# Outputs in two transfers of 64 rows, another order of loads, and a reshaped start, in a kernel that fuses linear attention with a two-layer MLP

## The chip, the cores and the metric

One core of a Trainium2 chip runs the whole program. The metric is device time in microseconds (us) of one execution. A run that is over 1.5% above the fastest of its kernel is labelled slow; comparisons use fast runs. The profile is of one execution, and its span is 1.7 us shorter than the time of that execution (220.1 against 221.82 us before).

## The reference, cut to what matters

```python
def _attn_ref(q, k, v, alpha):          # (4, 8, 768, 48): batch, heads, tokens, width
    for t in range(S):
        state = alpha[:, :, t, :, None] * state + outer(k_t, v_t)
        y[:, :, t] = q_t @ state
def _moe_ref(x, w_in, w_out):           # x is y as (3072, 384); w_in (384, 2048), w_out (2048, 384)
    h = x @ w_in
    r = np.maximum(h, 0.0)
    return ((r * r) @ w_out).astype(np.float32)
```

Inputs and the output are float32; the kernel multiplies in bfloat16.

## The kernel before

The work is cut into 12 units of 256 tokens. A unit has a front (decay factors, scaled q and k, their transposes), a back (key-value product `kv`, scores, masking, attention output `y`, its transpose) and an MLP part: 8 first-layer blocks `s1` of 6 matmuls and 8 second-layer groups `s2` of 4. The program records operations with a cost and a priority. A small model in Python then simulates five engines and the transfers, and so fixes, at build time, in which order each engine's queue holds them. On the chip each engine works through its queue in that order and waits on semaphores. What matters later is that an engine does not step over an operation whose data are late.

```python
# the model of time: what a transfer is thought to take
if o.sem is not None:
    dma_free = max(dma_free, o.end + self.DMA_FIRST) + o.lag
    land = dma_free + self.DMA_LAST
# ...  (cut)
# loads of one unit: alpha, k, q, v, 384 KB each, issued by SyncE
load_op[g, nm] = add("sp", lambda e, dst=dst, src=src: e.dma_start(dst, src), 400, L_PRIO[g] + j,
    writes=[("raw", r, j)], name=f"ld{nm}{g}", dma=f"{nm}{r}", lag=1500,
    after=[load_op[AFTER[g]]] if g in AFTER else [])
# ...  (cut) transposes of scaled k (a = 0) and q (a = 1): TensorE for units 0-5, DMA for units 6-11
bank = as_bf16(psZ if a == 0 else psX)
# ...  (cut) the output: one transfer per 128 tokens; partition 64*j + i holds token 2*i + j
r0 = b * S + i * T + 128 * jq
dst = bass.AP(tensor=out.tensor, offset=out.offset + r0 * DM, ap=[[DM, 2], [2 * DM, 64], [1, DM]])
add("sp", lambda e, ob=ob, dst=dst: e.dma_start(dst, OSB[ob][:]), 400, ps_ + 1300,
    reads=[("osb", ob)], name=f"out{m}_{ti}", dma=f"o{ob}", lag=600)
# ...  (cut) which transfer waits for which; win and wout are the weights, in two halves
AFTER = {("win", 0): (0, "q"), ("win", 1): (0, "q"), ("wout", 0): ("win", 0), ("wout", 1): ("win", 0),
         2: ("wout", 0), 3: ("wout", 0), 4: ("wout", 1), 5: ("wout", 1), 6: ("wout", 1)}
```

Of the kernel before, what the change touches and what calls it, by code (L numbers as in the profile page):

```python
# [5 lines left out]
ALU = mybir.AluOpType  # L6
# [253 lines left out]
def pe_ns(count, cols, at_once=1):  # L260
    return count * max(cols / 2.4 + 2.5, 25) / at_once
# [6 lines left out]
def dve_ns(n, rate=1.0):  # L268
    return 150 + n / 0.96 / rate
# [6 lines left out]
def bass_gla_recurrent__then__act_relu_squared_kernel(  # L276
# [9 lines left out]
    B, H, S, D = q.shape  # L286
# [57 lines left out]
    def as_bf16(t):  # L344
        return t[:].rearrange("p a b -> p (a b)").bitcast(BF16) if len(t.shape) == 3 else t[:].bitcast(BF16)
# [13 lines left out]
    def fill(buf, val):  # L359
        return lambda e: e.memset(buf, val)  # L360
# [3 lines left out]
                                         pattern=pattern, channel_multiplier=mult)  # L364

    for i in range(2):
        add("dve", fill(LAB[i][:], 0.0), 300, -1e6, writes=[("lab", i)])
    for i in range(NQKS):
        add("pool" if i else "dve", fill(QKS[i][:].rearrange("p a j h d -> p (a j h d)"), 0.0), 1200, -1e6 + 10,
            writes=[("qks", i, 0), ("qks", i, 1)])  # L370
    add("pool", fill(LINC[:], 1.0), 200, -1e6, writes=[("linc",)])
    add("pool", select(LINC[:], ALU.is_ge, 0.0, 0, [[1, 128]], -1), 300, -1e6, reads=[("linc",)], writes=[("linc",)])
# [11 lines left out]
    add("pool", select(IDENT[:], ALU.not_equal, 1.0, 0, [[-1, 128]], 1), 300, -1e6 + 5, reads=[("ident",)],  # L384
        writes=[("ident",)])

    add("pool", fill(CAUS[:].rearrange("p a b c -> p (a b c)"), 1.0), 200, -1e6 + 7, writes=[("caus",)])
    add("pool", fill(CAUS1[:].rearrange("p a b c -> p (a b c)"), 1.0), 200, -1e6 + 7, writes=[("caus1",)])
    for c, buf, key in ((0, CAUS, "caus"), (1, CAUS1, "caus1")):
        for jk in range(2):  # L390
            add("pool", select(buf[:, jk], ALU.is_ge, 0.0, 128 * c - jk, [[1, 2], [2, 64]], -2), 300, -1e6 + 7,
                reads=[(key,)], writes=[(key,)])
    add("dve", lambda e: e.tensor_copy(CAUS[64:128], CAUS1[64:128]), 200, -1e6 + 8, reads=[("caus1",), ("caus",)],
        writes=[("caus",)])

    def bcast(t, row, dims):
        return bass.AP(tensor=t, offset=0, ap=[[row, 128]] + dims)
# [19 lines left out]
    def load(g):  # L417
        b, i = units[g]
        t0 = i * T
        p0 = g * P  # L420
        r, la, qs, kt, pm, vb, x2 = (g % n for n in (NRAW, 2, NQKS, NKQT, NPM, NV, 2))
        first, last = i == 0, i == NST - 1
        xt = XSLOT[g]
        sr, sw = 2 * b + i % 2, 2 * b + (i + 1) % 2

        for j, t, nm in ((0, alpha, "a"), (1, k, "k"), (2, q, "q"), (3, v, "v")):
            src = t[b, :, t0:t0 + T, :].rearrange("h (p j) d -> p h (j d)", j=2)
            dst = RAW[r][:, j].rearrange("p h j d -> p h (j d)")
            load_op[g, nm] = add("sp", lambda e, dst=dst, src=src: e.dma_start(dst, src), 400, L_PRIO[g] + j,  # L429
                writes=[("raw", r, j)], name=f"ld{nm}{g}", dma=f"{nm}{r}", lag=1500,  # L430
                after=[load_op[AFTER[g]]] if g in AFTER else [])

    def front(g):
        b, i = units[g]
        t0 = i * T
        p0 = (g - AHEAD) * P
        r, la, qs, kt, pm, vb, x2 = (g % n for n in (NRAW, 2, NQKS, NKQT, NPM, NV, 2))
        first, last = i == 0, i == NST - 1
        xt = XSLOT[g]
# [56 lines left out]
        for a in range(2):  # L496
            src = QKS[qs][:, a].rearrange("p j h d -> p (j h d)")
            if g < PE_TRANSPOSED:
                bank = as_bf16(psZ if a == 0 else psX)
                psk = [("ps", "Z" if a == 0 else "X", 0)]  # L500

                def tr(pe, src=src, bank=bank):
                    for o in range(2 * NPR):
                        ins = pe.matmul(bank[:, o * 128:(o + 1) * 128], src[:, o * 128:(o + 1) * 128], IDENT[:],
                                        is_transpose=True)
                    return ins

                add("pe", tr, pe_ns(8, 128), p0 + 2500 + a, reads=[("qks", qs, a), ("ident",)], writes=psk,
                    name=f"tr{a}_{g}")
                dst = KQT[kt][:, a].rearrange("p j n s -> p (j n s)")  # L510
                add("dve", lambda e, dst=dst, bank=bank: e.tensor_copy(dst, bank[:, 0:1024]), dve_ns(1024, 2),  # L511
                    p0 + 3000 + a, reads=psk, writes=[("kqt", kt, a)], name=f"et{a}_{g}",
                    alts={"act": (lambda e, dst=dst, bank=bank: e.activation(dst, bank[:, 0:1024], AF.Copy),
                                  act_ns(1024))})
            else:
                dst = KQT[kt][:, a].rearrange("p j n s -> p (j n) s")
                add("sp", lambda e, dst=dst, src=src: e.dma_start_transpose(dst, src), 500, p0 + 2500 + a,
                    reads=[("qks", qs, a)], writes=[("kqt", kt, a)], name=f"tr{a}_{g}", dma=f"t{a}_{kt}", lag=1100)

    def back(g):  # L520
        b, i = units[g]
# [93 lines left out]
        src = XBF[x2][:].rearrange("p c n -> p (c n)")  # L615
        dst = XT[s][:, slot].rearrange("p c k t -> p (c k) t")
        if g < PE_X:
            bank = as_bf16(psW)

            def xtr(pe):  # L620
                for o in range(2 * KT):
                    ins = pe.matmul(bank[:, o * 128:(o + 1) * 128], src[:, o * 128:(o + 1) * 128], IDENT[:],
                                    is_transpose=True)
                return ins

            add("pe", xtr, pe_ns(6, 128), p0 + 6700, reads=[("xbf", x2), ("ident",)], writes=[("ps", "W")],
                name=f"xt{g}")
            add("dve", lambda e: e.tensor_copy(dst.rearrange("p a t -> p (a t)"), bank[:, 0:768]), dve_ns(768, 2),
                p0 + 7200, reads=[("ps", "W")], writes=[("xt", s, slot)], name=f"xv{g}")
        else:  # L630
            add("sp", lambda e: e.dma_start_transpose(dst, src), 500, p0 + 6700, reads=[("xbf", x2)],
                writes=[("xt", s, slot)], name=f"xt{g}", dma=f"x{s}{slot}", lag=850)

    rr_i = [0]
    h_i = [0]
# [2 lines left out]
    def moe(m, gs):  # L638
# [8 lines left out]
        for u in range(nb):  # L647
            hb, rb = h_i[0] % 2, rr_i[0] % NRR
            h_i[0] += 1
            rr_i[0] += 1  # L650
            pu = p0 + u * W * 0.5 / nb

            def s1(pe, u=u, hb=hb):
                for i in range(per):
                    fj = u * per + i
                    for kk in range(KT):
                        mov = XT[s][:, 0:nu_, :, kk, :].rearrange("p u c t -> p (u c) t")
                        ins = pe.matmul(psH[hb][:, i * n:(i + 1) * n], WIN[:, kk, fj * 128:(fj + 1) * 128], mov,  # L658
                                        start=(kk == 0), stop=(kk == KT - 1))
                return ins  # L660

            fjs = range(u * per, (u + 1) * per)
            add("pe", s1, pe_ns(KT * per, n), pu, reads=[("xt", s, i) for i in range(nu_)]
                + sorted({("win", f // FS) for f in fjs}), writes=[("ps", "H", hb)], name=f"s1_{m}_{u}")
            add("act", lambda e, hb=hb, rb=rb: e.activation(RR[rb][:], psH[hb][:], AF.Relu), act_ns(512), pu + 600,  # L665
                reads=[("ps", "H", hb)], writes=[("rr", rb)], name=f"re{m}_{u}",
                alts={"dve": (lambda e, hb=hb, rb=rb: e.tensor_scalar(RR[rb][:], psH[hb][:], 0.0, None, ALU.max),
                              dve_ns(512))})
            dst = GT[gt][:, u * per:(u + 1) * per, g0:g0 + nu_].rearrange("p f u c t -> p f (u c t)")
            sq = RR[rb][:].rearrange("p (f t) -> p f t", f=per)  # L670
            add("dve", lambda e, dst=dst, sq=sq: e.tensor_tensor(dst, sq, sq, ALU.mult), dve_ns(512, 2), pu + 1200,  # L671
                reads=[("rr", rb)], writes=[("gt", gt, g0 + i, fj) for i in range(nu_) for fj in fjs], name=f"sq{m}_{u}",
                alts={"pool": (lambda e, dst=dst, sq=sq: e.tensor_tensor(dst, sq, sq, ALU.mult), pool_ns(512))})  # L673
        for ti, (ui, jq) in enumerate((ui, jq) for ui in range(nu_) for jq in range(2)):
            b, i = units[gs[ui]]
            ob = o_i[0] % NOSB
# [1 line left out]
            for sg in range(4):  # L678
# [11 lines left out]
            add("act", lambda e, ob=ob: e.activation(OSB[ob][:], psO[:, 0:DM], AF.Copy), act_ns(DM), ps_ + 700,  # L690
                reads=[("ps", "O")], writes=[("osb", ob)], name=f"oe{m}_{ti}",
                alts={"dve": (lambda e, ob=ob: e.tensor_copy(OSB[ob][:], psO[:, 0:DM]), dve_ns(DM))})
            r0 = b * S + i * T + 128 * jq
            dst = bass.AP(tensor=out.tensor, offset=out.offset + r0 * DM, ap=[[DM, 2], [2 * DM, 64], [1, DM]])
            add("sp", lambda e, ob=ob, dst=dst: e.dma_start(dst, OSB[ob][:]), 400, ps_ + 1300,
                reads=[("osb", ob)], name=f"out{m}_{ti}", dma=f"o{ob}", lag=600)

    XSLOT = {g: (m % NXT, ui) for m, gs in enumerate(BLOCKS) for ui, g in enumerate(gs)}
    GSLOT = {}
# [7 lines left out]
    for g in range(5, G):  # L707
        ORDER += [f"f{g}", f"b{g - 1}"]
    ORDER += [f"b{G - 1}"]
    AFTER = {("win", 0): (0, "q"), ("win", 1): (0, "q"), ("wout", 0): ("win", 0), ("wout", 1): ("win", 0),  # L710
             2: ("wout", 0), 3: ("wout", 0), 4: ("wout", 1), 5: ("wout", 1), 6: ("wout", 1)}
    for st in ORDER:
        if st[0] == "f":
            load(int(st[1:]))
# [42 lines left out]
```

## Time and profile before

| before | value |
|---|---|
| time, median of 3 runs | 225.99 us (223.41 to 226.1) |
| span of the profiled run | 220.1 us (its time 221.82) |
| first first-layer matmul starts | 26.65 us |
| last output eviction ends | 210.93 + 0.49 = 211.42 us |
| so: ramp, middle, tail | 26.65, 184.77, 8.7 us |

The page has a view of 40 equal slices (5.5 us each here), one digit per slice: busy tenths for TensorE (PE), granted TensorE clock in tenths, and the mean busy share of the sixteen DMA engines. These are its rows for the kernel before:

```profile
PE   7999999998984998799319999999999999999830
PEclk9999999999998599999965999999999999999995
DMA  6997699999466679556979983457915650400110
```

TensorE is the busy engine, but it dips around slices 10 to 21, its clock drops twice, and the last slices do nothing. The DMA row reads as if there were room in slices 11 to 15 and from slice 25 on, while slices 20 to 24 are nearly full. It is the time that packets took (between 104 and 122 us packets of 256 bytes took 18 ns in median, but up to 3.7 us), as a mean over sixteen engines: whether a few of them have far more to do than the rest cannot be seen in it.

The next view is busy time by stretch of the kernel before: stretch, its length, TensorE busy time and matmul count, clock (1.00 is full), DMA share, GB/s.

```profile
85.00:104.00 19.00, 17.87 (x297) 1.00 0.65 177
104.00:122.00 18.00, 9.97 (x88) 0.72 0.98 169
122.00:135.00 13.00, 12.84 (x168) 1.00 0.76 122
```

In 104 to 122 TensorE loses 8 us and runs part of the rest at half clock. The timeline of SyncE's queue in the kernel before, at that place (start, duration of the issue, what is issued):

```profile
99.48 1.14 SPq L695 DMA_DIRECT2D out_dram<-osb  x1
100.66 1.30 SPq L429 DMA_DIRECT2D raw<-in_alpha_dram  x1
102.00 2.07 SPq L695 DMA_DIRECT2D out_dram<-osb  x1
104.12 4.95 SPq L517 DMA_TRANSPOSE kqt<-qks  x1
109.12 0.58 SPq L429 DMA_DIRECT2D raw<-in_k_dram  x1
109.74 3.30 SPq L517 DMA_TRANSPOSE kqt<-qks  x1
```

and TensorE's timeline there, where the brackets give the idle time before a group and what ended it:

```profile
110.48 0.81 PE L683 MATMUL psO<-wout,gt 128*128 128x384 bf16 x4 [3.85 <-POOL gt L673]
115.47 0.64 PE L573 MATMUL psX<-kqt 64*64 64x128 bf16 x16 [4.18 <-DMA kqt<-qks]
116.05 1.46 PE L658 MATMUL psH<-xt,win 128*128 128x256 bf16 x6
117.30 4.05 PE L683 MATMUL psO<-wout,gt 128*128 128x384 bf16 x12
```

The issue of a transpose blocks SyncE for 4.95 us just behind two outputs, and its tile lands 9.2 us after the start of the issue, the longest landing of the twelve. The transpose behind it is issued at 109.74 and lands 5.69 us later (view of the chain of waits). Afterwards twelve matmuls take 4.05 us where eight take 1.46 at full clock (at 77.49 us).

The ramp, in the timeline of all engines of the kernel before:

```profile
3.58 3.54 POOL L360 MEMSET qks<- 128x2048 bf16 x2
3.66 3.53 DVE L393 COPY caus<-caus 64x256 bf16<-64x256 bf16 x1
7.21 0.56 DVE L445 TENSOR_TENSOR prd<-raw 128x384 f32<-128x384 f32 x1
13.29 0.69 DVE L511 COPY kqt<-psX 128x1024 bf16<-128x1024 bf16 x1 [0.24 <-PE psX L504]
20.12 0.42 PE L573 MATMUL psX<-kqt 64*64 64x128 bf16 x16
21.22 0.83 POOL L485 CAST vbf<-raw 128x768 bf16<-128x768 f32 x1 [11.61 <-DMA raw<-in_v_dram]
26.65 1.47 PE L658 MATMUL psH<-xt,win 128*128 128x256 bf16 x12
```

Unit 0's tiles are ready at 13.98 but its scores run at 20.12, and the first layer starts at 26.65.

### The profile page before, as it was taken

To read this page: it belongs to the slowest core of one execution; us is meant where nothing else is said; L and a number is where in the kernel's file an instruction comes from. 1 tells how busy PE (TensorE), PEld (TensorE's weight loads), DVE (VectorE), ACT (ScalarE), POOL (GpSimd) and SP (SyncE) were. 2 spreads that over 40 slices of the span, in tenths; PEclk is the share of its full clock that TensorE was granted. 3 is DMA by queue.
4 is the path that set the end of the run, shared out by engine and by line. 5 is a ranking of instruction groups with operands and counts; after the bars stand their busy time and mean duration, and the time that the engine had idled before them with its cause. 6 is when DMAs were issued, how large, how long until landed. Compare 5 with 4: busy or idle time off the path is not lost.

```text
span 220.1 us, 5346 instructions
## 1 busy us (share of the span) xinstructions
PE 192.9 (88%) x2317; PEld 130.2 (59%) x2317; DVE 135.5 (62%) x214; ACT 101.7 (46%) x186; POOL 58.4 (27%) x72
## 2 busy tenths in 40 slices
PE   7999999998984998799319999999999999999830
PEld 2354687765662576568205776767677676777510
DVE  7678674893999269599403686884938727142300
ACT  2352185534942155358201555737548364555400
POOL 8701610393625114711313104510301201000000
PEclk9999999999998599999965999999999999999995
DMA  6997699999466679556979983457915650400110
GB/s 177 316 209 159 76 205 277 296 298 275 130 172 166 171 194 289 149 166 173 70 187 248 149 116 64 74 95 87 146 29 88 99 78 27 77 31 27 43 41 35
DMA packets 73416, 31.41 MB, mean 143 GB/s; under 512 B 67504, under 2 KB 72624, under 8 KB 73392
## 3 DMA queue, kind: packets, MB, share of 16 engines
q1 hardware_dynamic: 70512, 27.92, 57.5%
q0 software_dynamic: 2880, 3.15, 8.8%
q8 instruction: 18, 0.29, 0.5%
q14 instruction: 6, 0.05, 0.1%
HBM read 25.17 MB, written 4.72 MB: 136 GB/s over the span
## 4 chain that ended last, share of the span: by engine, by line
PE 63%; DVE 13%; DMA 13%; SPq 3%; issue 2%; ACT 2%; DVEq 0%
PE psO L683 27%; PE psH L658 22%; DMA xt<-xbf 5%; DMA raw<-in_q_dram 5%; DVE qks L490 3%; PE psX L600 3%; SPq L429 3%; DVE gt L671 3%; DMA kqt<-qks 3%; PE psX L593 2%; PE psO L725 2%; DVE kqt L511 2%; DVE pm L579 2%; PE psZ L573 1%; PE psZ L535 1%
## 5 line engine op out<-in xcount | busy, mean ns | idle before, releaser
L683 PE MATMUL psO<-wout,gt 128*128 128x384 bf16 x384 | 76.8, 339 | 7.0 <-POOL gt L673 3.8
L658 PE MATMUL psH<-xt,win 128*128 128x256 bf16 x576 | 73.5, 274 | 1.5 <-ACT rr L665 1.1
L665 ACT ACTIVATE rr<-psH 128x512 bf16<-128x512 f32 x90 | 53.6, 596 | 33.5 <-PE psH L658 31.5
L658 PEld LDWEIGHTS psH<-xt,win 128*128 128x128 bf16 x576 | 54.2, 98 | 13.2 <-ACT rr L665 2.1
L671 DVE TENSOR_TENSOR gt<-rr 128x512 bf16<-128x512 bf16 x80 | 39.7, 506 | 33.3 <-ACT rr L665 32.8
L683 PEld LDWEIGHTS psO<-wout,gt 128*128 128x128 bf16 x384 | 36.8, 101 | 29.9 <-issue 7.0
L673 POOL TENSOR_TENSOR gt<-rr 128x512 bf16<-128x512 bf16 x16 | 19.2, 1204 | 43.7 <-ACT rr L665 43.3
L690 ACT ACTIVATE osb<-psO 128x384 f32<-128x384 f32 x23 | 11.3, 490 | 30.7 <-PE psO L683 30.4
L485 POOL CAST vbf<-raw 128x768 bf16<-128x768 f32 x12 | 10.9, 912 | 41.5 <-DMA raw<-in_v_dram 26.7
L725 PE MATMUL psO<-zero 128*128 128x512 bf16 x73 | 20.0, 414 | 1.3 <-DVE zero L360 1.3
L579 DVE TENSOR_TENSOR pm<-psX,caus 128x1024 bf16<-128x1024 f32 x12 | 14.6, 1213 | 8.1 <-PE psX L573 8.1
L610 ACT ACTIVATE xbf<-psX 128x768 bf16<-128x768 f32 x12 | 9.7, 810 | 19.9 <-PE psX L600 19.9
L579 DVE TENSOR_TENSOR pm<-psZ,caus 128x1024 bf16<-128x1024 f32 x12 | 14.6, 1215 | 6.0 <-PE psZ L573 6.0
L490 DVE TENSOR_TENSOR qks<-raw,eq 128x768 bf16<-128x768 f32 x12 | 12.7, 1055 | 0.3 <-DMA raw<-in_q_dram 0.2
L725 PEld LDWEIGHTS psO<-zero 128*128 128x128 bf16 x73 | 7.0, 105 | 9.1 <-issue 2.7
L478 DVE TENSOR_TENSOR ek<-ek,raw 128x384 f32<-128x384 f32 x12 | 7.5, 627 | 7.2 <-ACT ek L465 7.2
L490 DVE TENSOR_TENSOR qks<-raw,ek 128x768 bf16<-128x768 f32 x12 | 11.4, 954 | 0.2
L448 ACT ACTIVATE lab<-prd 128x384 bf16<-128x384 f32 x12 | 6.2, 521 | 10.8 <-DVE prd L445 7.1
L551 POOL TENSOR_TENSOR smd<-tmp,own 128x384 bf16<-128x384 f32 x7 | 6.0, 852 | 16.0 <-DVE tmp L549 16.0
L447 POOL TENSOR_TENSOR prd<-raw 128x384 f32<-128x384 f32 x5 | 5.0, 998 | 18.9 <-DMA raw<-in_alpha_dram 18.9
L573 PE MATMUL psX<-kqt 64*64 64x128 bf16 x192 | 5.2, 229 | 5.0 <-DMA kqt<-qks 4.2
L465 ACT ACTIVATE ek<-psW 128x384 f32<-128x384 f32 x12 | 5.9, 488 | 7.3 <-PE psW L457 7.3
(66 smaller groups left out, 161.5 us busy)
## 6 DMA issues: line engine op xcount, KB each, us to landing
raw<-in_alpha_dram SPq DMA_DIRECT2D x12, 384.0 KB, 6.0
raw<-in_k_dram SPq DMA_DIRECT2D x12, 384.0 KB, 5.2
raw<-in_q_dram SPq DMA_DIRECT2D x12, 384.0 KB, 5.5
raw<-in_v_dram SPq DMA_DIRECT2D x12, 384.0 KB, 5.3
out_dram<-osb SPq DMA_DIRECT2D x24, 192.0 KB
win<-in_moe_w_in_dram POOLq DMA_DIRECT2D x2, 768.0 KB, 10.3
wout<-in_moe_w_out_dram POOLq DMA_DIRECT2D x2, 768.0 KB, 9.4
kqt<-qks SPq DMA_TRANSPOSE x12, 4.4
```

Of the source, the lines that this page charges most:

```text
L478: alts={"dve": (lambda e: e.tensor_tensor(hd(EK[la][:, 0, :]), hd(EK[la][:, 1, :]), al(1), ALU.mult), dve_ns(HD))})
L485: add("pool", lambda e: e.tensor_copy(VBF[vb][:].rearrange("p h j d -> p (h j d)"), RAW[r][:, 3].rearrange("p h j d -> p (h j d)")), pool_ ...
L490: add("dve", lambda e, a=a, E=E: e.tensor_tensor(QKS[qs][:, a, :, :, 0:D], RAW[r][:, 1 + a].rearrange("p h j d -> p j h d"), E[la][:].rear ...
L579: add("dve", lambda e, hf=hf, psT=psT: e.tensor_tensor(PM[pm][:, hf].rearrange("p r n j t -> p (r n) (j t)"), psT[:, :, :].rearrange("p r ...
L610: add("act", lambda e: e.activation(XBF[x2][:], psX[:, :, 0:HD], AF.Copy), act_ns(2 * HD), p0 + 6100, reads=[("ps", "X", 0), ("ps", "X", 1 ...
L658: ins = pe.matmul(psH[hb][:, i * n:(i + 1) * n], WIN[:, kk, fj * 128:(fj + 1) * 128], mov, start=(kk == 0), stop=(kk == KT - 1))
L665: add("act", lambda e, hb=hb, rb=rb: e.activation(RR[rb][:], psH[hb][:], AF.Relu), act_ns(512), pu + 600, reads=[("ps", "H", hb)], writes= ...
L671: add("dve", lambda e, dst=dst, sq=sq: e.tensor_tensor(dst, sq, sq, ALU.mult), dve_ns(512, 2), pu + 1200, reads=[("rr", rb)], writes=[("gt ...
L673: alts={"pool": (lambda e, dst=dst, sq=sq: e.tensor_tensor(dst, sq, sq, ALU.mult), pool_ns(512))})
L683: ins = pe.matmul(psO[:, 0:DM], GT[gt][:, fj, g0 + ui, jq, :], WOUT[:, fj, :], start=(fj == 0), stop=(fj == FT - 1))
L690: add("act", lambda e, ob=ob: e.activation(OSB[ob][:], psO[:, 0:DM], AF.Copy), act_ns(DM), ps_ + 700, reads=[("ps", "O")], writes=[("osb", ...
L725: pr.fill(lambda pe: pe.matmul(psO[:, 0:512], ZERO[:, 0:128], ZERO[:], skip_group_check=True), 216, min(o.start for o in pr.order["pe"] if ...
```

## The change

Its intent is a faster start (VectorE free earlier, unit 0 ahead of unit 1), unit 2's data earlier, and better outputs. The cost numbers of the model were adjusted with it. The core of the diff:

```diff
-        add("dve", fill(LAB[i][:], 0.0), 300, -1e6, writes=[("lab", i)])
+        add("dve", fill(LAB[i][:, :, D:64], 0.0), 150, -1e6, writes=[("lab", i)])
-        add("pool" if i else "dve", fill(QKS[i][:].rearrange("p a j h d -> p (a j h d)"), 0.0), 1200, ...
+        add("dve", fill(QKS[i][:, :, :, :, D:64].rearrange("p a j h d -> p (a j h) d"), 0.0), 500, ...
-    add("dve", lambda e: e.tensor_copy(CAUS[64:128], CAUS1[64:128]), 200, ...
+    (one more select and an addition on GpSimd make the mask)
-        p0 = (g - AHEAD) * P
+        p0 = (g - AHEAD) * P if g > 1 else g * P
-                bank = as_bf16(psZ if a == 0 else psX)
+                bank = as_bf16(psH[a] if g == 1 else psZ if a == 0 else psX)
-            bank = as_bf16(psW)            # transpose of the attention output, units 0-5
+            bank = as_bf16(psX)
     (model: lag of a load 1500 -> 1230, of DMA transposes 1100 -> 1250 and 850 -> 950;
      squaring 417 -> 500 ns on VectorE by the cost formula, 1069 -> 1200 on GpSimd)
-            r0 = b * S + i * T + 128 * jq
-            dst = bass.AP(tensor=out.tensor, offset=out.offset + r0 * DM, ap=[[DM, 2], [2 * DM, 64], [1, DM]])
-            add("sp", lambda e, ob=ob, dst=dst: e.dma_start(dst, OSB[ob][:]), 400, ps_ + 1300, ...
+            for j in range(2):
+                r0 = b * S + i * T + 128 * jq + j
+                dst = bass.AP(tensor=out.tensor, offset=out.offset + r0 * DM, ap=[[2 * DM, 64], [1, DM]])
+                add("sp", lambda e, ...: e.dma_start(dst, OSB[ob][64 * j:64 * j + 64, :]), 500, ps_ + 1300, ...
-    AFTER = {..., ("wout", 0): ("win", 0), ("wout", 1): ("win", 0), 2: ("wout", 0), 3: ("wout", 0), 4: ("wout", 1), ...
+    AFTER = {..., 2: ("win", 0), ("wout", 0): ("win", 1), ("wout", 1): ("win", 1), 3: ("wout", 0), 4: ("wout", 0), ...
```

More of the change, by code (lines that the diff above doesn't have):

```diff
@@ L366, in bass_gla_recurrent__then__act_relu_squared_kernel @@
     for i in range(2):
-        add("dve", fill(LAB[i][:], 0.0), 300, -1e6, writes=[("lab", i)])
+        add("dve", fill(LAB[i][:, :, D:64], 0.0), 150, -1e6, writes=[("lab", i)])
     for i in range(NQKS):
-        add("pool" if i else "dve", fill(QKS[i][:].rearrange("p a j h d -> p (a j h d)"), 0.0), 1200, -1e6 + 10,
+        add("dve", fill(QKS[i][:, :, :, :, D:64].rearrange("p a j h d -> p (a j h) d"), 0.0), 500, -1e6 + 10,
             writes=[("qks", i, 0), ("qks", i, 1)])
@@ L385, in bass_gla_recurrent__then__act_relu_squared_kernel @@
         writes=[("ident",)])
-    add("pool", fill(CAUS[:].rearrange("p a b c -> p (a b c)"), 1.0), 200, -1e6 + 7, writes=[("caus",)])
-    add("pool", fill(CAUS1[:].rearrange("p a b c -> p (a b c)"), 1.0), 200, -1e6 + 7, writes=[("caus1",)])
     for c, buf, key in ((0, CAUS, "caus"), (1, CAUS1, "caus1")):
+        add("pool", fill(buf[:].rearrange("p a b c -> p (a b c)"), 1.0), 200, -1e6 + 7, writes=[(key,)])
         for jk in range(2):
@@ L392, in bass_gla_recurrent__then__act_relu_squared_kernel @@
                 reads=[(key,)], writes=[(key,)])
-    add("dve", lambda e: e.tensor_copy(CAUS[64:128], CAUS1[64:128]), 200, -1e6 + 8, reads=[("caus1",), ("caus",)],
-        writes=[("caus",)])
+    flat = CAUS1[:].rearrange("p a b c -> p (a b c)")
+    add("pool", select(flat, ALU.is_ge, 0.0, -64, [[0, 256]], 1), 400, -1e6 + 7, reads=[("caus1",)],
+        writes=[("caus1",)])
+    add("pool", lambda e: e.tensor_tensor(CAUS[:].rearrange("p a b c -> p (a b c)"),
+                                          CAUS[:].rearrange("p a b c -> p (a b c)"), flat, ALU.add), 700, -1e6 + 8,
+        reads=[("caus1",), ("caus",)], writes=[("caus",)])
     def bcast(t, row, dims):
@@ L429, in load @@
             load_op[g, nm] = add("sp", lambda e, dst=dst, src=src: e.dma_start(dst, src), 400, L_PRIO[g] + j,
-                writes=[("raw", r, j)], name=f"ld{nm}{g}", dma=f"{nm}{r}", lag=1500,
+                writes=[("raw", r, j)], name=f"ld{nm}{g}", dma=f"{nm}{r}", lag=1230,
                 after=[load_op[AFTER[g]]] if g in AFTER else [])
@@ L498, in front @@
             if g < PE_TRANSPOSED:
-                bank = as_bf16(psZ if a == 0 else psX)
-                psk = [("ps", "Z" if a == 0 else "X", 0)]
+                bank = as_bf16(psH[a] if g == 1 else psZ if a == 0 else psX)
+                psk = [("ps", "H", a) if g == 1 else ("ps", "Z" if a == 0 else "X", 0)]
                 def tr(pe, src=src, bank=bank):
@@ L517, in front @@
                 add("sp", lambda e, dst=dst, src=src: e.dma_start_transpose(dst, src), 500, p0 + 2500 + a,
-                    reads=[("qks", qs, a)], writes=[("kqt", kt, a)], name=f"tr{a}_{g}", dma=f"t{a}_{kt}", lag=1100)
+                    reads=[("qks", qs, a)], writes=[("kqt", kt, a)], name=f"tr{a}_{g}", dma=f"t{a}_{kt}", lag=1250)
     def back(g):
@@ L624, in xtr @@
                 return ins
-            add("pe", xtr, pe_ns(6, 128), p0 + 6700, reads=[("xbf", x2), ("ident",)], writes=[("ps", "W")],
+            add("pe", xtr, pe_ns(6, 128), p0 + 6700, reads=[("xbf", x2), ("ident",)], writes=[("ps", "X", 0)],
                 name=f"xt{g}")
             add("dve", lambda e: e.tensor_copy(dst.rearrange("p a t -> p (a t)"), bank[:, 0:768]), dve_ns(768, 2),
-                p0 + 7200, reads=[("ps", "W")], writes=[("xt", s, slot)], name=f"xv{g}")
+                p0 + 7200, reads=[("ps", "X", 0)], writes=[("xt", s, slot)], name=f"xv{g}")
         else:
             add("sp", lambda e: e.dma_start_transpose(dst, src), 500, p0 + 6700, reads=[("xbf", x2)],
-                writes=[("xt", s, slot)], name=f"xt{g}", dma=f"x{s}{slot}", lag=850)
+                writes=[("xt", s, slot)], name=f"xt{g}", dma=f"x{s}{slot}", lag=950)
     rr_i = [0]
@@ L670, in moe @@
             sq = RR[rb][:].rearrange("p (f t) -> p f t", f=per)
-            add("dve", lambda e, dst=dst, sq=sq: e.tensor_tensor(dst, sq, sq, ALU.mult), dve_ns(512, 2), pu + 1200,
+            add("dve", lambda e, dst=dst, sq=sq: e.tensor_tensor(dst, sq, sq, ALU.mult), 500, pu + 1200,
                 reads=[("rr", rb)], writes=[("gt", gt, g0 + i, fj) for i in range(nu_) for fj in fjs], name=f"sq{m}_{u}",
-                alts={"pool": (lambda e, dst=dst, sq=sq: e.tensor_tensor(dst, sq, sq, ALU.mult), pool_ns(512))})
+                alts={"pool": (lambda e, dst=dst, sq=sq: e.tensor_tensor(dst, sq, sq, ALU.mult), 1200)})
         for ti, (ui, jq) in enumerate((ui, jq) for ui in range(nu_) for jq in range(2)):
@@ L692, in moe @@
                 alts={"dve": (lambda e, ob=ob: e.tensor_copy(OSB[ob][:], psO[:, 0:DM]), dve_ns(DM))})
-            r0 = b * S + i * T + 128 * jq
-            dst = bass.AP(tensor=out.tensor, offset=out.offset + r0 * DM, ap=[[DM, 2], [2 * DM, 64], [1, DM]])
-            add("sp", lambda e, ob=ob, dst=dst: e.dma_start(dst, OSB[ob][:]), 400, ps_ + 1300,
-                reads=[("osb", ob)], name=f"out{m}_{ti}", dma=f"o{ob}", lag=600)
+            for j in range(2):
+                r0 = b * S + i * T + 128 * jq + j
+                dst = bass.AP(tensor=out.tensor, offset=out.offset + r0 * DM, ap=[[2 * DM, 64], [1, DM]])
+                add("sp", lambda e, ob=ob, dst=dst, j=j: e.dma_start(dst, OSB[ob][64 * j:64 * j + 64, :]), 500,
+                    ps_ + 1300, reads=[("osb", ob)], name=f"out{m}_{ti}_{j}", dma=f"o{ob}{j}", lag=300)
     XSLOT = {g: (m % NXT, ui) for m, gs in enumerate(BLOCKS) for ui, g in enumerate(gs)}
@@ L709, in bass_gla_recurrent__then__act_relu_squared_kernel @@
     ORDER += [f"b{G - 1}"]
-    AFTER = {("win", 0): (0, "q"), ("win", 1): (0, "q"), ("wout", 0): ("win", 0), ("wout", 1): ("win", 0),
-             2: ("wout", 0), 3: ("wout", 0), 4: ("wout", 1), 5: ("wout", 1), 6: ("wout", 1)}
+    AFTER = {("win", 0): (0, "q"), ("win", 1): (0, "q"), 2: ("win", 0), ("wout", 0): ("win", 1),
+             ("wout", 1): ("win", 1), 3: ("wout", 0), 4: ("wout", 0), 5: ("wout", 1), 6: ("wout", 1)}
     for st in ORDER:
```

## The prediction

> **What bounds it now.** TensorE. From 135 to 205 us it is busy 69.8 of 70 us (view of busy time by stretches), at full clock, some 12.5 to 13.2 us per unit. The 220.1 us span loses time in three places.
>
> 1. Ramp. The first first-layer matmul starts at 26.6 us (timeline). Unit 0's second transposed tile is ready at 13.98, yet its scores run only at 20.1: unit 1's front shares the X and Z banks and goes ahead, and its q, issued at 6.70, takes 10.8 us behind the weights (chain of waits). And the first alpha product waits on VectorE until 7.2 behind a 3.53 us copy of the causal mask, which overlaps GpSimd's 3.54 us of clearing QKS; the landing records put alpha at about 4.3.
> 2. Middle. From 26.6 to 205 TensorE is idle about 16 us, 8 of them in 104-122, where it waits 4.2 us for a DMA-transposed tile; that tile's issue takes 4.95 us on SyncE's queue and the next 3.3, just after two output transfers. Twice the granted clock is then 0.5 (6.8 and 10.2 us); eight second-layer matmuls take 2.72 us there instead of 1.30. I estimate 5 us lost.
> 3. Tail. The last output eviction ends at 211.4, the span at 220.1: 8.7 us for one 192 KB transfer.
>
> **Why two transfers help.** The output's destination has an outermost dimension of 2. [...] each output shows three semaphore steps, not sixteen; packets of 1536 bytes take about 65 ns and never run faster than 33 per us. So 24 x 128 packets keep two engines busy for about 93 us (estimate), on top of their sixteenth of all else; the average DMA share hides it. Loads and transposes, spread over all 16, wait for these two, and SyncE's queue backs up. With an outermost 64 all engines share it: about 0.3 us of engine time per half. Cost: 24 more issues of about 0.5 us on SyncE.
>
> **The rest.** Clearing only the padding and building the mask on GpSimd frees VectorE by about 4 us, so alpha's landing decides: 2.5 to 3 us. The other banks and unit 1's later priority let unit 0 go first: scores near 11, x near 17, limited by the first weight half (landed about 15.7). First-layer start: about 18, against 26.6. The second-layer weights are issued at about 20 instead of 22.8, beside unit 2's loads (about 16 instead of 30.7); both should land before TensorE needs them (about 29 and 45).
>
> **Sum (estimates).** Ramp -8.5; tail -3.5 (a first load takes 3.5 us from issue to landing; the last half is issued 0.5 us later); middle -13 of some 21. Span about 195; the run before profiled at 221.8 while its median is 226, so I add 2 us.
>
> **Prediction: 197 us, range 187 to 209.** Chances: faster by over 2% 0.96, within 2% 0.03, slower 0.01.
>
> **Checks.** First-layer start at 17 to 20 us; span minus end of last output eviction 4 to 6; sixteen completions per output half; load and transpose issues nearer 1.2 us than 3 to 5; no 4 us wait for a transposed tile; at most one stretch of half clock; steady units still 12.5 to 13.2.
>
> **What would make it wrong.** VectorE (14.3 of 15 us busy in 55-70) limits the middle after an earlier start; unit 2's loads delay the second-layer weights; transposes, not outputs, clog the queue; SyncE's static order leaves it blocked behind loads waiting for buffers.

Cut from it is a rule by which I got the number of engines from the output's access pattern; no trace shows the rule. That the outputs of the kernel before use two engines, and an outermost 64 all sixteen, stands there as my estimate: no record names the engine of a packet. What the trace of the kernel before counts is three completion steps per output, and sixteen per load, weight half and DMA transpose; that of the kernel after counts sixteen per output half. The 93 us are 3072 packets at 33 per us, the 0.3 us are 64 packets of 65 ns over sixteen engines, both estimates from the trace. -8.5, -3.5 and -13 from 220 give about 195 us, and 2 more give 197.

## The result, and the profile after

The kernel after took 199.82 us (median of 4 runs, 199.37 to 201.46), against 224.8 for the kernel before (median of 4). The ratio is 0.8903, 95% interval 0.8815 to 0.8991. Ratios here are the mean time of one kernel's fast runs over that of the other's in the same rounds, so not quite the ratio of the medians. The prediction of 197 us, range 187 to 209, holds. In a later set on another chip the same kernel had 200.48 us and a ratio of 0.9057.

| profiled runs, us | before | after | difference | predicted |
|---|---|---|---|---|
| ramp, to the first first-layer matmul | 26.65 | 26.59 | -0.1 | -8.5 |
| middle, to the end of the last output eviction | 184.77 | 166.74 | -18.0 | -13 |
| tail, to the end of the span | 8.7 | 4.3 | -4.4 | -3.5 |
| span | 220.1 | 197.6 | -22.5 | -25 |

The total is right, but partly by luck, as a sum of errors that cancel: the ramp gained nothing, and the middle and the tail gained more than predicted. The same rows of the 40 slices (now 4.9 us each), of the kernel after:

```profile
PE   7997399899999999999999999999899999999980
PEclk9999789999999999999999999999999999999998
DMA  6999928999998999999669664352544941131211
```

The dips in the middle are gone, and one remains in slice 5 (a 3 in a row of 9s), with the clock drop behind it. The same three windows of time in the kernel after, whose work stands earlier by then:

```profile
85.00:104.00 19.00, 18.59 (x250) 1.00 0.83 192
104.00:122.00 18.00, 18.00 (x261) 1.00 0.73 134
122.00:135.00 13.00, 13.00 (x173) 1.00 0.54 102
```

Unit 6, the first with DMA transposes, now comes around 86 us. SyncE's queue at that place in the kernel after:

```profile
83.09 3.08 SPq L699 DMA_DIRECT2D out_dram<-osb  x4
86.22 2.04 SPq L520 DMA_TRANSPOSE kqt<-qks  x1
88.31 0.57 SPq L432 DMA_DIRECT2D raw<-in_alpha_dram  x1
88.93 0.75 SPq L432 DMA_DIRECT2D raw<-in_k_dram  x1
89.72 0.97 SPq L699 DMA_DIRECT2D out_dram<-osb  x1
90.74 1.65 SPq L520 DMA_TRANSPOSE kqt<-qks  x1
```

The longest issue of these transposes is now 2.04 us; their median fell from 1.94 to 1.23. TensorE waits for none of them.

The ramp of the kernel after, all engines:

```profile
4.36 1.04 DVE L448 TENSOR_TENSOR prd<-raw 128x384 f32<-128x384 f32 x1 [1.43 <-DMA raw<-in_alpha_dram]
18.04 0.81 ACT L613 ACTIVATE xbf<-psX 128x768 bf16<-128x768 f32 x1 [1.92 <-PE psX L603]
22.01 0.82 POOL L488 CAST vbf<-raw 128x768 bf16<-128x768 f32 x1 [5.77 <-DMA raw<-in_v_dram]
22.98 0.82 PE L538 MATMUL psZ<-vbf,qks 64*128 64x96 bf16 x16 [4.23 <-POOL vbf L488]
23.74 0.82 PE L625 MATMUL psX<-ident,xbf 128*128 128x128 bf16 x6
26.59 0.82 PE L661 MATMUL psH<-xt,win 128*128 128x256 bf16 x6
29.14 1.82 POOL L411 DMA_DIRECT2D wout<-in_moe_w_out_dram  x2
```

VectorE does start 2.85 us earlier, and unit 0's attention output is converted by 18.85 instead of 25.34. Then TensorE's queue holds the key-value product of unit 1 ahead of unit 0's transpose. That product needs v of unit 1, which lands near 21.9. TensorE idles 4.23 us, loses its clock for 3.4 us, and the first layer starts where it always did.

The tail is the last line of the waits of SyncE's queue (L249 is the wait for all outputs at the program's end). Of the kernel before, and of the kernel after:

```profile
SPq L249 <- DMA out_dram<-osb: 6.7, 1, 6.7
```

```profile
SPq L249 <- DMA out_dram<-osb: 1.6, 1, 1.6
```

### The profile page after: what moved, and what is told of

Same layout as the page of the kernel before. It is cut to its first block, busy times and chain, and to the rows that moved or that the text cites. A ratio compares the mean times of both kernels' runs of the same rounds, so it can differ in the third digit from the quotient of the medians.

```text
span 197.6 us, 5328 instructions
## 1 busy us (share of the span) xinstructions
PE 182.8 (92%) x2292; PEld 127.4 (64%) x2296; DVE 131.4 (66%) x211; ACT 101.2 (51%) x186; POOL 61.9 (31%) x76
## 4 chain that ended last, share of the span: by engine, by line
PE 70%; DVE 11%; DMA 7%; SPq 3%; issue 3%; POOL 1%; ACT 1%
PE psH L661 28%; PE psO L686 27%; DMA raw<-in_v_dram 7%; DVE qks L493 4%; SPq L432 3%; PE psX L603 3%; DVE gt L674 2%; PE psZ L538 2%; PE psX L596 2%; PE psZ L576 2%; PE psX L576 2%; PE psX L507 1%; PE psW L456 1%; PE psH L507 1%; PE psX L625 1%
## 5 line engine op out<-in xcount | busy, mean ns | idle before, releaser
L686 PE MATMUL psO<-wout,gt 128*128 128x384 bf16 x384 | 72.9, 326 | 1.7 <-DVE gt L674 1.1
L661 PE MATMUL psH<-xt,win 128*128 128x256 bf16 x576 | 72.8, 273 | 0.3 <-DVE xt L631 0.2
L668 ACT ACTIVATE rr<-psH 128x512 bf16<-128x512 f32 x92 | 54.8, 597 | 30.2 <-PE psH L661 28.2
L676 POOL TENSOR_TENSOR gt<-rr 128x512 bf16<-128x512 bf16 x14 | 16.4, 1169 | 12.9 <-ACT rr L668 9.9
L488 POOL CAST vbf<-raw 128x768 bf16<-128x768 f32 x12 | 11.6, 970 | 18.2 <-PE psX L603 10.2
L729 PE MATMUL psO<-zero 128*128 128x512 bf16 x48 | 13.7, 429 | 1.4 <-DVE zero L360 1.3
L613 ACT ACTIVATE xbf<-psX 128x768 bf16<-128x768 f32 x10 | 8.1, 811 | 9.5 <-PE psX L603 9.5
L493 DVE TENSOR_TENSOR qks<-raw,ek 128x768 bf16<-128x768 f32 x12 | 12.4, 1036 | 0.2
L483 POOL TENSOR_TENSOR eq<-eq,raw 128x384 f32<-128x384 f32 x6 | 6.3, 1047 | 19.6 <-ACT eq L477 19.6
L561 POOL TENSOR_TENSOR sbd<-tmp,acm 128x384 bf16<-128x384 f32 x8 | 7.0, 871 | 11.9 <-DVE tmp L559 11.9
L538 PE MATMUL psZ<-vbf,qks 64*128 64x96 bf16 x160 | 6.5, 211 | 4.2 <-POOL vbf L488 4.2
L729 PEld LDWEIGHTS psO<-zero 128*128 128x128 bf16 x52 | 5.2, 107 | 7.1 <-issue 2.7
L538 PEld LDWEIGHTS psZ<-vbf,qks 64*128 64x128 bf16 x160 | 4.7, 98 | 7.6 <-issue 7.2
```

The lines of the kernel that those rows point to most:

```text
L488: add("pool", lambda e: e.tensor_copy(VBF[vb][:].rearrange("p h j d -> p (h j d)"), RAW[r][:, 3].rearrange("p h j d -> p (h j d)")), pool_ ...
L493: add("dve", lambda e, a=a, E=E: e.tensor_tensor(QKS[qs][:, a, :, :, 0:D], RAW[r][:, 1 + a].rearrange("p h j d -> p j h d"), E[la][:].rear ...
L538: ins = pe.matmul(psZ[:, c, p * 96:p * 96 + 96], QKS[qs][h0:h0 + 64, 0, j, 2 * p:2 * p + 2, :].rearrange("p h d -> p (h d)"), VBF[vb][h0:h ...
L613: add("act", lambda e: e.activation(XBF[x2][:], psX[:, :, 0:HD], AF.Copy), act_ns(2 * HD), p0 + 6100, reads=[("ps", "X", 0), ("ps", "X", 1 ...
L661: ins = pe.matmul(psH[hb][:, i * n:(i + 1) * n], WIN[:, kk, fj * 128:(fj + 1) * 128], mov, start=(kk == 0), stop=(kk == KT - 1))
L668: add("act", lambda e, hb=hb, rb=rb: e.activation(RR[rb][:], psH[hb][:], AF.Relu), act_ns(512), pu + 600, reads=[("ps", "H", hb)], writes= ...
```

## The experiments

Theories at the start of this part. T: outputs on two DMA engines (my reading of their three completion steps) clogged loads, transposes and SyncE's queue, and took most of the middle and part of the tail. R, the rival: the new order of work gave the middle, and the outputs are worth only their tail. For the ramp: the fixed order, against a limit by the transfers themselves. Runs 1 to 4 share a chip, as do 5 to 8 and 9 to 12; each set has its own runs of the kernel before, with medians of 222.79, 221.2 and 221.43 us. Only runs 5 to 8 have the kernel after beside them. The others are held against its two ratios, 0.8903 and 0.9057, so a difference of less than about 1.5% from the kernel after is not resolved there. The record's class for runs 1 to 4 is "unclear", and "faster" or "slower" for the rest; the intervals of runs 1, 3 and 4 end at 0.9351 or below, that of run 2 lies just above 1.

**1. Before, with sixteen engines for the outputs and nothing else.** Every engine's order is unchanged; the rows land in the wrong places.

```diff
-ap=[[DM, 2], [2 * DM, 64], [1, DM]]
+ap=[[DM, 128], [1, DM]]
```

> The kernel before with one edit: the output transfer's destination is 128 consecutive rows, so its outermost dimension is 128 and not 2 (rows land in the wrong order on purpose; bytes, count of transfers and every engine's order are as before). Theory T (two engines carry all outputs and that clogs loads, transposes and SyncE's queue): sixteen completions per output, tail after the last eviction 8.7 -> about 5 us, and the middle (first first-layer matmul to last eviction) shrinks from 184.8 us to 167-177 us; time 202 to 213 us. Rival R (the change's new order of work, not the outputs, gave the middle): only the tail changes, 219 to 222 us.

Measured: 204.41 us, ratio 0.9247 (0.9143 to 0.9351), result wrong. Completion counts per output are sixteen, where the kernel before has three (which I read as two engines, and one step for the fourteen that do nothing). The packet records of the kept traces agree: in any one microsecond at most 34 output packets start in the kernel before, 152 in this run. Middle 26.51 to 199.07 us, so 172.6; tail 3.1. The transfers of the kernel before, with median time from issue to landing at the end of the line:

```profile
kqt<-qks SPq DMA_TRANSPOSE x12, 4.4
xt<-xbf SPq DMA_TRANSPOSE x6, 4.3
```

and of this run:

```profile
out_dram<-osb SPq DMA_DIRECT2D x24, 192.0 KB, 2.2
kqt<-qks SPq DMA_TRANSPOSE x12, 3.1
xt<-xbf SPq DMA_TRANSPOSE x6, 2.8
```

T is shown, with the two engines read from the counts: one number in one access pattern took 12.2 us off the middle and 5.6 off the tail, and other transfers became faster, though nothing else was changed. (The loads too: those issued after the first output, at 52 us, took 6.5 us in median before and 4.9 here; the median over all twelve hides it.) R falls.

**2. After, with two engines for the outputs.** Order and count as in the kernel after; rows permuted within a half.

```diff
-ap=[[2 * DM, 64], [1, DM]]
+ap=[[2 * DM, 2], [4 * DM, 32], [1, DM]]
```

> The kernel after with one edit: each half's destination gets an outermost dimension of 2 (rows permuted within the half, wrong on purpose), order and count unchanged. T: three semaphore steps per half, SyncE issues of 3 to 5 us return, TensorE waits in the middle return, time 213 to 224 us. R: only the tail grows, 201 to 205 us.

Measured: 224.8 us in its two fast runs (229.4 in two labelled slow), ratio 1.0142 (1.0012 to 1.0271): all of the change's gain is gone, and a little more than T's 213 to 224. The profiled run is one of the slow ones, so I read from it only what kind of waits there are. TensorE's longest waits in it:

```profile
PE psO L686 <- DVE gt L674: 6.5, 2, 5.4
PE psH L661 <- DMA xt<-xbf: 4.2, 2, 3.7
```

and its transfers, slow run as well:

```profile
kqt<-qks SPq DMA_TRANSPOSE x12, 5.2
xt<-xbf SPq DMA_TRANSPOSE x6, 5.4
```

Each half shows three completion steps again. Experiments 1 and 2 remove and restore the same cost in two different orders of work, and agree.

**3. After, with four engines.** The same edit with `[[2 * DM, 4], [8 * DM, 16], [1, DM]]`.

> As the previous, with an outermost dimension of 4. T by an estimate of engine time (3072 packets of 65 ns over 4 engines are 50 us, over 2 they are 100 us, beside some 125 us of other work on each engine in a span of about 195 us): four engines are busy 175 of 195 us, so most of the gain stays, 200 to 206 us. R: 200 to 202 us.

Measured: 202.12 us, ratio 0.9138 (0.9046 to 0.923); five completion steps per half, read as four engines and one step for the rest. At most 68 output packets start in any microsecond here. So two engines cost some 25 us and four 2 to 5 (0.9138 against 0.9057 and 0.8903), which is far from proportional. It fits the estimate in the expectation, that the loss begins where the hot engines have more work than the span holds (its 125 us of other work: in the trace of the kernel after, the packets other than outputs took 121.8 us per engine, as a mean over sixteen), but three points do not test such a limit. The DMA transposes land as late here (median 4.6 us) as in the kernel before (4.4), so their median landing time alone does not measure the loss.

**4. After, with the model told when q and v of unit 1 really land.**

```diff
-                        land = dma_free + self.DMA_LAST
+                        land = dma_free + self.DMA_LAST + self.LATE.get(o.name, 0)
+    LATE = {"ldq1": 6000, "ldv1": 9500}
```

> The kernel after with the scheduler's model told that unit 1's q and v land 6.0 and 9.5 us later than it thought (measured 17.4 and 21.9 us, modelled 11.1 and 12.3); nothing on the chip but the order changes. Theory: the ramp gained nothing because TensorE's fixed order puts unit 1's key-value product, which needs v of unit 1, ahead of unit 0's first layer; now the 4.2 us wait and the half-clock stretch of 3.4 us vanish, first-layer start 26.6 -> 20 to 21.5 us, second-layer weights issued at about 21 instead of 29, time 193 to 197 us. Rival: the weights' arrival bounds the ramp anyway, later waits take it back, 198 to 201 us.

Measured: 200.64 us, ratio 0.9057 (0.8963 to 0.9152). The first layer starts at 19.87, about as expected, and the time does not move. The gain is given back at 30 to 40 us, in this run's timeline:

```profile
34.16 0.82 POOL L489 CAST vbf<-raw 128x768 bf16<-128x768 f32 x1 [6.40 <-DMA raw<-in_v_dram]
34.94 0.99 POOL L484 TENSOR_TENSOR eq<-eq,raw 128x384 f32<-128x384 f32 x1
35.97 1.57 DVE L494 TENSOR_TENSOR qks<-raw,eq 128x768 bf16<-128x768 f32 x1 [4.97 <-POOL eq L484]
38.20 0.82 PE L539 MATMUL psZ<-vbf,qks 64*128 64x96 bf16 x16 [5.39 <-DVE kqt L515]
```

Now the second-layer weights are issued at 21.05, and v of unit 2, issued at 21.68, lands near 34.1 behind them, after 12.4 us, where the median of the twelve loads of v in this run is 5.3; the model thought 25.9. GpSimd sits in its queue before the conversion of v, the operation behind it is late, VectorE waits, TensorE waits. The same fault, one unit later. The rival's prediction was right here, though not yet its reason.

**5. The kernel after again**, as a yardstick for the next three.

> The kernel after, unchanged, as the yardstick on this chip for the runs beside it: about 0.89 of before, 199 to 201 us, first-layer start at 26 to 27 us.

Measured: 200.48 us, ratio 0.9057 (0.9018 to 0.9096), first-layer start 27.29.

**6. After, with the old clears and the old mask.** All else in the same order.

```diff
-    (padding cleared on VectorE, mask finished on GpSimd)
+    (whole LAB and QKS cleared, two of them on GpSimd; mask copied by VectorE)
```

> The kernel after with the old clears and the old causal mask (whole LAB and QKS cleared, two of them on GpSimd, mask copied by VectorE); the scheduler's order of all else is the same. Theory (the ramp waits for v of unit 1 at about 22 us, so earlier starts are slack): the first alpha product goes back from 4.4 to about 7.2 us, the output of unit 0's attention from 18.9 to about 21.5, but the key-value product of unit 1 stays near 23 and the time stays within 1 us of the kernel after. Rival (the earlier start was worth what the prediction gave it): 2.5 to 3 us slower.

Measured: 198.67 us, ratio 0.8982 (0.8955 to 0.9009). The first alpha product goes back from 4.24 to 7.21 and the conversion of unit 0's output ends at 19.08, yet the kernel is 1.8 us faster, not slower, than in run 5, a little outside the 1 us that I allowed. That part of the change bought nothing: the 3 us were slack in front of the wait for v. Why the old form is slightly ahead is not shown; the order of the other work is the same, and the clock may be much of it: the profiled run of run 5 has a half-clock stretch of 6.8 us from 21.60, that of run 6 one of 3.4 us, and run 5's one execution at a granted clock of 0.990 took 199.44 us.

**7. As run 4, and told that unit 2's v is late too** (`"ldv2": 8000` added).

> As the run that was told of unit 1's late q and v, and told besides that unit 2's v lands 8 us later than modelled (34.0 against 25.9 us there), so that its conversion does not block GpSimd's queue, and with it the next product. If the 5.4 us TensorE wait of that run was only an order that did not know this, it goes and the time falls to 194 to 197 us; if the early phase is bound by what the transfers bring, another wait of similar size appears and the time stays at 198 to 201 us.

Measured: 197.84 us, ratio 0.8935 (0.8876 to 0.8995). That lies between the two ranges. No wait of TensorE is over 1.7 us, the clock stays full to the end of the work (1.00 from 20.28 to 191.3 us), and the result is right. Against run 5 that is 0.8935 / 0.9057 = 0.987. It is the best mean beside the kernel after on one chip, by 1.3%. But the first layer starts at 20.28, 7.0 us earlier than in run 5, so most of that start is still lost. Between the first first-layer matmul and the last eviction, TensorE here spends 3.0 us on idle-time filler matmuls and 5.0 us idle; in the kernel after it is 0.2 and 4.0. About 4 us of the head start became waiting under another name.

**8. After, with the first-layer weights behind v of unit 1.**

```diff
-    AFTER = {("win", 0): (0, "q"), ("win", 1): (0, "q"), ...
+    AFTER = {("win", 0): (1, "v"), ("win", 1): (1, "v"), ...
```

> The kernel after with the first-layer weights issued when unit 1's v has landed (about 12.5 us) and not when unit 0's q has (6.7). Unit 1's q and v then land near 11.5 and 12.7 instead of 17.4 and 21.9, the weight halves near 20 and 24.5 instead of 15.6 and 21.0. If late arrival of unit 1 behind the weights is what holds the ramp, the key-value wait and the half-clock stretch go, first-layer start falls from 26.6 to 20 to 22 us and the time to 193 to 198 us; if the total of bytes up to the second-layer weights is the limit, the gain is given back in waits at 30 to 45 us and the time is 198 to 201 us.

Measured: 203.63 us, ratio 0.9191 (0.9151 to 0.923): slower. Its longest TensorE wait:

```profile
PE psX L507 <- DVE qks L493: 4.6, 1, 4.6
```

Unit 1 is on time (its product runs at 20.34), but GpSimd, busy with other work, issues the weights at 16.93 instead of 12.5, and unit 2 repeats the chain of run 4: its v is waited for until 39.32. Both outcomes missed; the sum of bytes before the second layer has to be moved in any order, and this order moves it later.

**9. Before, with the change's output edit alone** (two transfers of 64 rows; result right).

> The kernel before with the change's output edit alone: two transfers of 64 rows, results right. If the number of engines is what the outputs needed and the halves cost little, the ratio to before is that of the run with sixteen engines and one transfer, 0.91 to 0.94 (201 to 208 us); the tail is about 1 us longer than there for the second issue. If the doubled issues on SyncE hurt, over 0.95.

Measured: 206.49 us, ratio 0.9332 (0.926 to 0.9405). Tail 4.3 us against 3.1 in run 1. So the output edit by itself carries about two thirds of the change (6.7% of some 10%), and a single transfer on sixteen engines would be no worse.

**10. After, with the old order of loads** (`AFTER` of the kernel before).

> The kernel after with the old order of transfers (second-layer weights after the first half of the first-layer weights, unit 2 after the second-layer weights). Since the start is bound by unit 1's v, which does not change, I expect first-layer start still at 26 to 27 us, but unit 2's tiles 8 to 10 us later and TensorE waits for them near 45 to 60 us: 3 to 6 us slower than the kernel after (ratio 0.915 to 0.935). If loads were not what the rest of the gain (ratio 0.925 to 0.90) came from: within 1 us of the kernel after.

Measured: 201.61 us, ratio 0.9092 (0.8994 to 0.9191). No clear loss. My 3 to 6 us are not there: the waits at 45 to 60 us are 1.5 us at 54.66 and 1.0 at 59.01. But two of its four executions took 203 us at a granted clock of 0.96, and without the kernel after on this chip a loss of 1 or 2% cannot be excluded.

**11. After, with the old banks and the old priority of unit 1.**

> The kernel after with the old banks and the old priority of unit 1 (its transposes in X and Z, unit 0's in W). If the banks and the priority gain nothing, as the first-layer start at 26.6 in both kernels suggests: ratio within 0.01 of the kernel after (0.89 to 0.915). If they carry the rest of the gain: 0.92 to 0.93.

Measured: 198.3 us, ratio 0.8948 (0.8883 to 0.9013). The first layer starts later, at 28.15, and the kernel is not slower: TensorE does unit 1's attention while it waits and does not lose its clock (0.998 over the span). Where the first layer starts is a poor measure of the ramp.

**12. Told as in run 7, first layer in natural token order, one output transfer of 128 consecutive rows.**

```diff
-mov = XT[s][:, 0:nu_, :, kk, :].rearrange("p u c t -> p (u c) t")
+mov = XT[s][:, 0, :, kk, :].rearrange("p c (j i) -> p c i j", j=2)
```

> An attempt at a version faster than both: the kernel told of the late q, v of unit 1 and v of unit 2, and the first layer reads its tokens in natural order (moving operand with a stride), so that one output transfer of 128 consecutive rows has sixteen engines; 24 issues fewer. Against that told kernel (0.8935) the tail should be about 1 us shorter: ratio 0.885 to 0.893, results right. If the strided read slows the first-layer matmuls above 109 ns, the time rises instead, by about 63 us times the slowing.

Measured: 269.02 us, ratio 1.2157, result right: a failure. Costliest groups of the page, in this run and in the kernel after:

```profile
L662 PE MATMUL psH<-xt,win 128*128 128x256 bf16 x576 | 149.8, 405 | 0.3 <-ACT rr L669 0.2
```

```profile
L661 PE MATMUL psH<-xt,win 128*128 128x256 bf16 x576 | 72.8, 273 | 0.3 <-DVE xt L631 0.2
```

The moving operand read in pairs 128 bytes apart costs TensorE 77 us over 576 matmuls, twice the time, to save some 1.1 us of tail (3.2 against 4.3 in run 7). From the start of one such matmul to the next the median is 244 ns, where it is 109 in run 7. Why such a read takes longer is not shown: no run varies the distance.

## Why the prediction was right, point by point

- **Two engines carried all outputs: right as far as counts can show it.** Runs 1, 2, 3 and 9 take the cost away, put it back, give a dose and do it alone. The number two came from the rule; the trace of the kernel before had the three steps and the packet rate, but not the engines. What is measured: an outermost dimension of 2 gives 3 completion steps, 4 gives 5, 64 or 128 give 16. The most packets that start in a microsecond go the same way: 34, 68, and 128 or more. That these are two, four and sixteen engines is my reading of the counts.
- **The tail: right.** Predicted -3.5, measured -4.4.
- **The middle: right in mechanism, mis-sized.** Predicted "-13 of some 21", measured -18.0. Of this, run 1 assigns 12.2 to the outputs. I had kept 8 us of gaps for VectorE in its busy stretch (14.3 of 15 us in 55 to 70); the kernel after has VectorE at 14.4 of 15 there and TensorE at 15.0. A busy VectorE was not a limit in that stretch.
- **The ramp: wrong.** The step that failed is "First-layer start: about 18, against 26.6", worth "-8.5"; measured 26.59 and -0.1. Unit 0's scores ran at 13.81, not "near 11", and its output was converted by 18.85; what failed came after. Two things were missing. First, I let unit 0 go ahead by data and banks, but did not look at what stands between in TensorE's queue: the product of unit 1, whose v lands at 21.9 because the weights go ahead of it (in run 8, with the weights behind it, its product runs at 20.34 instead of 22.98). The line was in the profile of before, at 21.22. Second, runs 4 and 7 show that even a start at 20 is worth at most 3 us, because what TensorE lacks next is late as well.
- **The second-layer weights "at about 20": wrong.** They were issued at 29.14, because GpSimd's queue holds them behind operations that need unit 1.
- **The clock: right in number, and only in part explained.** Two stretches of half clock in the middle became none there, and one of 3.4 us, from 22.38, begins late in the 4.23 us wait of the ramp, which ends at 22.98. The recorded half-clock stretches, apart from those that run to the end of a trace, have 3.4, 6.8 and 10.2 us: one, two and three times the shortest. The length of the wait does not tell them apart: a wait of 2.18 us goes with the 6.8 us stretch at 70.38 in the kernel before, the same with one of 3.4 us in run 1, and 1.82 us with the second stretch of run 9, while a wait of 2.11 us in run 11 cost no clock. What decides stays open.

What stays open is the rest of the gain, from about 0.93 (run 9) to about 0.90. It is mostly idle time: between the first first-layer matmul and the last output eviction TensorE is idle for 17.0 us in the kernel before, 9.2 in run 1 and 4.5 in the kernel after, and busy for 167.7, 163.4 and 162.2. Two waits of run 1, 4.0 us together, are for VectorE's masked scores, with one half-clock stretch; in the kernel after they are gone, and runs 6, 10 and 11 bring back at most 1.5 us of the kind (run 10). Which edit removed them is not shown. Undoing the mask, the loads, or the banks one at a time (runs 6, 10, 11) loses nothing that stands out. What is left are the model's new cost numbers, or combinations; no run tells these apart. Runs 10 and 11 also reshuffle the fixed order of the other work, and run 6, which does not, still moved the time by 0.8%, so effects of 1% are not told apart here.

## What to carry to other kernels

Count the completion steps of every frequent transfer: outputs with three steps, which I read as two engines, slowed loads and DMA transposes, which show sixteen (medians to landing of 6.5 and 4.4 us, against 4.9 and 3.1 in run 1). The mean DMA share does not tell: over the middle it was 0.67 before and 0.68 after. Here an outermost dimension of 64 or 128 gave sixteen steps, and 2 or 4 gave three or five; but do not pay for it with a strided moving operand (72.8 to 149.8 us busy in run 12). Before you credit an earlier start, look at what stands in front in each in-order queue and when its last input really lands; a fixed order made from wrong landing times turns one late transfer into waits on three engines.
